# Fewer warm-up products and a drain placed elsewhere, in a kernel of attention and expert routing

## The chip, the cores and the metric

The kernel runs on one core of one Trainium2 chip. The core has five engines with instruction queues of their own: TensorE (PE in the profile; its loads of the stationary operand are PEld), VectorE (DVE), ScalarE (ACT), GpSimd (POOL) and SyncE (SP, which here only starts transfers). They wait for each other through semaphores. The metric is the time of one execution in microseconds of the device; less is better.

## The reference

A linear attention over four batches of four heads, 1088 positions and 32 features, whose output, laid out as 4352 tokens of 128 features, goes through a layer of eight experts, of which each token uses the one with the highest score.

```python
def _attn_ref(q, k, v, S1, S2):
    def phi(x):                                   # 64 features from two sketches of 8
        a = np.einsum('rd,bhsd->bhsr', S1, x)
        b = np.einsum('rd,bhsd->bhsr', S2, x)
        return np.einsum('bhsi,bhsj->bhsij', a, b).reshape(*x.shape[:-1], r * r)
    q_p, k_p = (phi(q), phi(k))
    kv = np.einsum('bhsf,bhsd->bhfd', k_p, v)
    z = np.sum(k_p, axis=2)
    num = np.einsum('bhsf,bhfd->bhsd', q_p, kv)
    den = np.einsum('bhsf,bhf->bhs', q_p, z)[..., None] + 1e-06
    return (num / den)

def _moe_ref(x, w_gate, w1, w2):                  # x: 4352 tokens x 128
    logits = x @ w_gate
    expert_idx = np.argmax(logits, axis=1)
    ...                                           # gate_w: the softmax at the chosen expert
    for e in range(E):
        mask = expert_idx == e
        out[mask] = gate_w[mask, None] * (np.maximum(x[mask] @ w1[e], 0.0) @ w2[e])
    return out
```

All in float32.

## The kernel before

The program has two parts. In the first, TensorE transposes blocks of keys and queries, multiplies them with the sketches, sums keys times values and forms the tokens; POOL scatters the tokens into a table in DRAM (`xs_dram`), sorted by expert. In the second, 34 tiles (`JMIN`) of up to 128 tokens of one expert, and up to four optional ones of two half tiles, are gathered back, go through the expert's two products (`up`, `down`) and are stored to their places in the output by POOL.

The beginning, as far as it matters here. Loads go out on two queues; meanwhile TensorE multiplies zeros:

```python
    nc.vector.memset(zeros, 0.0)
    # ... loads of the sketches, of keys, values and queries ...
    idle = bank_ps("idle")
    for i in range(12):
        nc.tensor.matmul(idle[:, 0:128], lhsT=zeros[:, 0:128], rhs=zeros[:, 0:128], start=True, stop=True)
    # ... VectorE unpacks the sketches (given as float64) into s_rep ...

    def finish_s():                       # first of the order: two transposes of the sketches
        for i in range(2):
            nc.tensor.transpose(p[:, :2 * R], in_=sT[i]..., identity=ident[:2 * R, :2 * R])
            # ... VectorE: s_cat

    def features(name, n, srcs, dst):     # T.K00, T.K01, ...: then the first blocks of keys
        def turn():
            for i, s in enumerate(srcs()):
                nc.tensor.transpose(tp[:, ts(i, 128)], in_=s, identity=ident)
            nc.scalar.copy(out=st["xT"][:, :n * 128], in_=tp[:, :n * 128])
        def project():
            # ... TensorE: xT times s_cat, ScalarE, VectorE: the 64 features
```

The weights of the experts (16 loads of 512 KB) follow on SP's queue while the first part runs.

The store of a tile, an indirect transfer that POOL issues, and the loop over the tiles (five of them are done before it):

```python
    def down(j):
        # ... TensorE: py = hT times w2 of the tile's expert
        y = y_of(j)                       # sixteen buffers
        nc.scalar.activation(y, py[:, :DM], AF.Copy, bias=0.0, scale=xg_of(j)[:, DM:DM + 1])

    def store(j):
        d = nc.gpsimd.indirect_dma_start(
            out=out[:], out_offset=bass.IndirectOffsetOnAxis(ap=to_of(j), axis=0),
            in_=y_of(j), in_offset=None, bounds_check=NTOK - 1, oob_is_err=False)

    for j in range(5, JMIN):
        o = after.get(j)                  # an optional tile beside tiles 14, 18, 22, 26
        if o is not None:
            with tc.If(runs[o - JMIN] > 0) as found:
                # ... x_in(j + 2), up(o), down(j), up(j + 1), down(o)
            with found.Else():
                # ... the same without o
            waiting += [j, o]
        else:
            # ... x_in(j + 2), up(j + 1), down(j)
            waiting.append(j)
        # ... gathers of later tiles
        for _ in range(2 if j + 1 < JMIN else JT):
            if waiting:
                store(waiting.pop(0))
        if j % 8 == 0 and j > 8 or j + 3 == JMIN:
            nc.gpsimd.drain()
```

With `JMIN` = 34 the drain stands behind the stores of tiles 16, 24, 31 and 32. In the profile `idle` is line 198, the store line 856, y line 852, the drain line 949, the branch line 915, and line 976 is the end of the program.

Of the kernel before, what the change touches and what calls it, by code (L numbers as in the profile page):

```python
# [62 lines left out]
def kernel(  # L63
# [31 lines left out]
    JMIN = NTOK // 128  # L95
# [26 lines left out]
    def bank_ps(name):  # L122
        return ps_w.tile([128, 512], FP, tag="w", name=name)
# [70 lines left out]


    idle = bank_ps("idle")
    for i in range(12):
        nc.tensor.matmul(idle[:, 0:128], lhsT=zeros[:, 0:128], rhs=zeros[:, 0:128], start=True, stop=True)  # L198


# [583 lines left out]
    def gather(j):  # L784
        n = 128 // len(tiles[j][0])
        for i, (_, at) in enumerate(tiles[j][0]):
            _, (row,) = nc.values_load_multi_w_load_instructions(
                at, engines=[mybir.EngineType.SP], min_val=0, max_val=E * NTOK - n,
                skip_runtime_bounds_check_because="the table keeps a tile within its expert's rows")
            d = nc.sync.dma_start(out=xg_of(j)[ts(i, n)].bitcast(I32), in_=xs_dram[ds(row, n), :])  # L790
            if j < JE:
                tc.declare_no_dep(d.ins, group="late", reason="late rows are in no tile of the first group")
                tc.add_to_no_dep_group("early", d.ins)
# [7 lines left out]
    def x_in(j):  # L801
        xg = xg_of(j)
        xTp = bank_ps(f"xgTp{j}")
        nc.tensor.transpose(xTp[:, :128], in_=xg[:, 0:DM], identity=ident)  # L804
        nc.scalar.copy(out=xT_of(j), in_=xTp[:, :128])  # L805
        for w1, (at, _) in zip([w1_of(j)] if j < JMIN else w1_half, tiles[j][0]):
            wo = w_offset(at, DVE)
            nc.vector.tensor_copy(out=w1, in_=w1_all[:, ds(wo, F)])  # L808
        if j >= JMIN:

            nc.vector.tensor_copy(out=w2_half, in_=w2_all[:, ds(wo, F)])

    def rows_out(j):

        to = to_of(j)
        row_id = xg_of(j)[:, DM + 1:DM + 2].bitcast(I32)
        if j < JE:
            nc.vector.tensor_copy(out=to, in_=row_id)
        else:
            nc.vector.tensor_tensor(to, row_id, tiles[j][1], ALU.bitwise_or)  # L820

    def up(j):
        xT = xT_of(j)
        ph = wide_ps(f"ph{j}")
        for c in range(NFC):
            if j < JMIN:
                nc.tensor.matmul(ph[:, ts(c, 128)], lhsT=w1_of(j)[:, ts(c, 128)], rhs=xT, start=True, stop=True)  # L827
                continue
            for i, w1 in enumerate(w1_half):
                for m in range(2):  # L830
                    nc.tensor.matmul(ph[ts(m, 64), ds(c * 128 + i * 64, 64)], lhsT=w1[:, ds(c * 128 + m * 64, 64)],  # L831
                                     rhs=xT[:, ts(i, 64)], start=True, stop=True)
        hT = hT_of(j)
        nc.scalar.activation(hT[:, 0:512], ph[:, 0:512], AF.Relu)  # L834
        if j <= 7:

            nc.scalar.activation(hT[:, 512:1024], ph[:, 512:1024], AF.Relu)
        else:
            nc.vector.tensor_scalar(hT[:, 512:1024], ph[:, 512:1024], 0.0, None, ALU.max)  # L839

    def down(j):
        hT = hT_of(j)
        wo = w_offset(tiles[j][0][0][0], PE)
        n = 128 // len(tiles[j][0])
        py = bank_ps(f"py{j}")
        for c in range(NFC):
            for i in range(128 // n):
                nc.tensor.matmul(py[ts(i, n), :DM], lhsT=hT[:, ds(c * 128 + i * n, n)],  # L848
                                 rhs=w2_half[:, ts(c, DM)] if i else w2_all[:, ds(wo + c * DM, DM)],
                                 start=(c == 0), stop=(c == NFC - 1))  # L850
        y = y_of(j)
        nc.scalar.activation(y, py[:, :DM], AF.Copy, bias=0.0, scale=xg_of(j)[:, DM:DM + 1])  # L852

    def store(j):
        y = y_of(j)
        d = nc.gpsimd.indirect_dma_start(  # L856
            out=out[:], out_offset=bass.IndirectOffsetOnAxis(ap=to_of(j), axis=0),
            in_=y, in_offset=None, bounds_check=NTOK - 1, oob_is_err=False)
        tc.declare_no_dep(d.ins, group="y", reason="every token is in one tile")
        tc.add_to_no_dep_group("y", d.ins)  # L860
# [18 lines left out]
    def piece():  # L879
        for _ in last_table:  # L880
            break
# [21 lines left out]
    for j in range(sum(name[0] == "Z" for name in begun), JMIN):  # L903
        o = after.get(j)
        if j + 4 == min(after):
            runs = []
            for i in range(NS):
                _, (v,) = nc.values_load_multi_w_load_instructions(
                    tiles["runs"][0:1, i:i + 1], engines=engines, min_val=0, max_val=2 * NS,
                    skip_runtime_bounds_check_because="a number of halves")  # L910
                runs.append(v)
        if o is not None:
            rows_out(j)
            rows_out(o)
            with tc.If(runs[o - JMIN] > 0) as found:
                x_in(j + 2)
                up(o)
                down(j)
                up(j + 1)
                down(o)  # L920
            with found.Else():
                up(j + 1)
                x_in(j + 2)
                down(j)
            waiting += [j, o]
        else:
            if j + 2 < JMIN:
                x_in(j + 2)
            if j + 1 in after:
                x_in(after[j + 1])  # L930
            rows_out(j)
            if j + 1 < JMIN:
                up(j + 1)
            for _ in range({5: 8, 6: 4}.get(j, 0)):
                piece()
            down(j)
            waiting.append(j)

        for i in range(JE, j + AHEAD + 1) if j == 6 else [j + AHEAD] if j > 6 else []:
            if i < JMIN:  # L940
                gather(i)
        if j > 8 and optional:
            gather(optional.pop(0))
        for _ in range(2 if j + 1 < JMIN else JT):
            if waiting:
                store(waiting.pop(0))
        if j % 8 == 0 and j > 8 or j + 3 == JMIN:

            nc.gpsimd.drain()  # L949

# [30 lines left out]
```

## Time and profile before

| | |
|---|---|
| time, median of 3 | 227.0 us (226.95 to 227.46) |
| span of the profiled execution | 252.5 us |
| mean granted clock of TensorE in it | 0.912 |
| TensorE busy | 214.7 us, 85% |
| VectorE, ScalarE, POOL busy | 113.8, 75.3, 84.0 us |
| moved by DMA | 23.15 MB |

The span runs from the first to the last instruction of one profiled execution; it is longer than the plain ones, which have no profile. A group of instructions is named by its line, its engine, its operation and its tiles as `out<-in`. "Issue" is idle time that no release in the profile explains. An engine's name with a q (POOLq, PEldq) is its sequencer: waits, branches and drains stand there and do not count as busy. In a table of windows each line is a stretch in us, then its length, the engine's busy time with the number of instructions, the granted clock (1.00 is full), the busy share of the DMA engines and GB/s. By the page, POOL's stores are 34 instructions of 979 ns, and 34 scatters of 1011 ns stand before them.

### The profile page before, as it was taken

What the parts mean: (1) busy time and instruction counts of PE and PEld (TensorE: products, weight loads), DVE (VectorE), ACT (ScalarE), POOL (GpSimd) and SP (SyncE); (2) the same over time, 40 slices, a digit from 0 to 9 for tenths busy, and PEclk for the clock granted to TensorE, in tenths of its full rate; (3) what the DMA queues carried; (4) which work ended last, traced back from release to release, by engine and by line L of the source; (5) the groups of instructions that cost most, each with busy time, mean ns of one, the idle gap of its engine ahead of it and who ended that gap; (6) DMA issues with size and microseconds to landing.
All of it is one profiled execution on the core that took longest, in us unless ns stands there. A gap on an engine that the chain in (4) does not pass through costs nothing.

```text
span 252.5 us, 7067 instructions
## 1 busy us (share of the span) xinstructions
PE 214.7 (85%) x2654; PEld 204.4 (81%) x2654; DVE 113.8 (45%) x310; ACT 75.3 (30%) x197; POOL 84.0 (33%) x130
## 2 busy tenths in 40 slices
PE   8998995595599895991099999999999999799990
PEld 8888993583498795990099999899999999699990
DVE  4565882361268770185081344533632555153320
ACT  2546370041145322400043323222232233132220
POOL 6440057337400084077422321304114333133322
PEclk9999999598589998696579999999999999799997
DMA  5988688888831221011112211101101111000000
GB/s 172 323 229 175 179 247 253 257 234 235 276 101 25 63 66 42 3 44 53 42 31 76 64 44 45 43 4 49 32 14 46 34 32 32 14 12 22 10 23 21
DMA packets 28180, 23.15 MB, mean 92 GB/s; under 512 B 5786, under 2 KB 26012, under 8 KB 28144
## 3 DMA queue, kind: packets, MB, share of 16 engines
q1 hardware_dynamic: 24736, 18.02, 26.1%
q0 software_dynamic: 2304, 4.50, 5.3%
q8 instruction: 25, 0.41, 0.7%
q10 hardware_dynamic: 1104, 0.13, 0.4%
q14 instruction: 11, 0.09, 0.1%
HBM read 17.61 MB, written 5.29 MB: 91 GB/s over the span
## 4 chain that ended last, share of the span: by engine, by line
PE 72%; issue 12%; another core or an unknown queue 7%; DVE 3%; ACT 2%; POOLq 1%; SPq 1%; DMA 1%; POOL 0%; DVEq 0%; ACTq 0%
PE ph L827 23%; PE py L848 22%; PE ab_K L356 4%; PE ab_Q L356 4%; PE kv L379 3%; PE nd_Q L454 3%; PE qp_Q L442 2%; PE idle L198 2%; PE tp_Q L347 2%; PE ph L831 2%; PE xgTp L804 1%; PE tp_K L347 1%; POOLq L949 1%; DMA x_rows<-xs_dram 1%
## 5 line engine op out<-in xcount | busy, mean ns | idle before, releaser
L827 PE MATMUL ph<-xgT,w 128*128 128x128 f32 x544 | 71.9, 287 | 15.6 <-ACT xgT L805 9.5
L827 PEld LDWEIGHTS ph<-xgT,w 128*128 128x128 f32 x544 | 68.1, 202 | 17.1 <-ACT xgT L805 10.7
L848 PE MATMUL py<-w_all,hT 128*128 (+1 forms) x576 | 72.5, 280 | 1.6 <-issue 1.6
L848 PEld LDWEIGHTS py<-w_all,hT 128*128 128x128 f32 (+1 forms) x576 | 68.8, 193 | 2.3 <-issue 1.8
L856 POOL DMA_INDIRECT out_dram<-y,to x34 | 33.3, 979 | 92.9 <-ACT xgT L805 61.1
L550 POOL DMA_INDIRECT xs_dram<-x_rows,row_i x34 | 34.4, 1011 | 49.1 <-DVE base_e L544 21.8
L839 DVE TENSOR_SCALAR hT<-ph 128x512 f32<-128x512 f32 x28 | 19.4, 692 | 67.0 <-ACT hT L834 55.6
L834 ACT ACTIVATE hT<-ph 128x512 f32<-128x512 f32 x36 | 21.6, 599 | 58.1 <-PE ph L827 39.6
L852 ACT ACTIVATE y<-py,x_rows 128x128 f32<-128x128 f32 x34 | 12.5, 368 | 56.1 <-PE py L848 34.7
L808 DVE COPY w<-w_all 128x1024 f32 x34 | 23.3, 691 | 10.9 <-remote 8.3
L356 PE MATMUL ab_Q<-s_cat,xT_Q 128*64 128x64 f32 x256 | 12.9, 232 | 8.0 <-issue 8.0
L356 PEld LDWEIGHTS ab_Q<-s_cat,xT_Q 128*64 128x64 f32 x256 | 10.6, 142 | 9.5 <-issue 9.5
L356 PE MATMUL ab_K<-s_cat,xT_K 128*64 128x64 f32 x256 | 11.4, 235 | 3.4 <-issue 3.1
L364 DVE TENSOR_TENSOR q_p_Q<-half_Q 128x1024 f32<-128x1024 f32 x8 | 9.7, 1224 | 10.3 <-ACT half_Q L363 10.3
L356 PEld LDWEIGHTS ab_K<-s_cat,xT_K 128*64 128x64 f32 x256 | 9.7, 146 | 4.9 <-issue 4.4
L364 DVE TENSOR_TENSOR k_p<-half_K 128x1024 f32<-128x1024 f32 x8 | 9.6, 1221 | 6.8 <-issue 4.1
L454 PE MATMUL nd_Q<-kvx,q_pT_Q 128*64 128x82 f32 x256 | 11.4, 237 | 1.4 <-issue 1.3
L454 PEld LDWEIGHTS nd_Q<-kvx,q_pT_Q 128*64 128x64 f32 x256 | 10.0, 136 | 2.7 <-issue 2.2
L230 POOL COPY v_aug<-v 128x1024 f32<-128x1024 f32 x4 | 5.5, 1386 | 19.0 <-DMA v<-in_v_dram 19.0
L804 PE MATMUL xgTp<-ident,x_rows 128*128 128x128 f32 x38 | 10.2, 286 | 0.3 <-issue 0.3
L805 ACT COPY xgT<-xgTp 128x128 f32<-128x128 f32 x38 | 9.4, 264 | 2.8 <-PE xgTp L804 1.6
L363 ACT COPY half_Q<-ab_Q 128x256 f32<-128x256 f32 x8 | 3.0, 373 | 24.4 <-PE ab_Q L356 18.3
(194 smaller groups left out, 213.6 us busy)
## 6 DMA issues: line engine op xcount, KB each, us to landing
w_all<-in_moe_w_dram SPq DMA_DIRECT2D x16, 512.0 KB
x_rows<-xs_dram SPq DMA_DIRECT2D x34, 65.0 KB
k<-in_k_dram SPq DMA_DIRECT2D x4, 512.0 KB
v<-in_v_dram SPq DMA_DIRECT2D x4, 512.0 KB
q<-in_q_dram SPq DMA_DIRECT2D x4, 512.0 KB
xs_dram<-x_rows,row_i POOLq DMA_INDIRECT x34
out_dram<-y,to POOLq DMA_INDIRECT x34
xs_dram<-zeros SPq DMA_DIRECT2D x1, 520.0 KB
```

What stands on the lines that cost most here:

```text
L356: nc.tensor.matmul(ab[ts(m, 64)].rearrange("p (g i r) -> p g i r", g=4, i=n)[:, :, i], lhsT=st["xT"][:, ds(i * 128 + m * 64, 64)], rhs=s_c ...
L364: nc.vector.tensor_tensor(f.rearrange("p g (a b) -> p g a b", a=R), half[:, :, 0:R, None].broadcast_to(shape), half[:, :, None, R:2 * R].b ...
L454: nc.tensor.matmul(nd[ts(m, 64), i, ds(hp * 2 * KC, 2 * KC)], lhsT=t[:, ds((i * NP + hp) * 128 + m * 64, 64)], rhs=kvx[bs[m]][:, hp].rearr ...
L550: d = nc.gpsimd.indirect_dma_start(out=xs_dram[:], out_offset=bass.IndirectOffsetOnAxis(ap=row_i[:, u:u + 1], axis=0), in_=x[:, u, :].bitc ...
L804: nc.tensor.transpose(xTp[:, :128], in_=xg[:, 0:DM], identity=ident)
L808: nc.vector.tensor_copy(out=w1, in_=w1_all[:, ds(wo, F)])
L827: nc.tensor.matmul(ph[:, ts(c, 128)], lhsT=w1_of(j)[:, ts(c, 128)], rhs=xT, start=True, stop=True)
L834: nc.scalar.activation(hT[:, 0:512], ph[:, 0:512], AF.Relu)
L839: nc.vector.tensor_scalar(hT[:, 512:1024], ph[:, 512:1024], 0.0, None, ALU.max)
L848: nc.tensor.matmul(py[ts(i, n), :DM], lhsT=hT[:, ds(c * 128 + i * n, n)], rhs=w2_half[:, ts(c, DM)] if i else w2_all[:, ds(wo + c * DM, DM ...
L852: nc.scalar.activation(y, py[:, :DM], AF.Copy, bias=0.0, scale=xg_of(j)[:, DM:DM + 1])
L856: d = nc.gpsimd.indirect_dma_start(out=out[:], out_offset=bass.IndirectOffsetOnAxis(ap=to_of(j), axis=0), in_=y, in_offset=None, bounds_ch ...
```

## The change

Two edits. TensorE multiplies zeros eight times at the start in place of twelve; the products fill the time until the first keys are there. And the drains of POOL among the tiles stand behind tiles 14, 22 and 30 (`JMIN - 4`) in place of 16, 24, 31 and 32, so that there are three of them, the last one four tiles from the end.

```diff
     idle = bank_ps("idle")
-    for i in range(12):
+    for i in range(8):
         nc.tensor.matmul(idle[:, 0:128], lhsT=zeros[:, 0:128], rhs=zeros[:, 0:128], start=True, stop=True)
...
             if waiting:
                 store(waiting.pop(0))
-        if j % 8 == 0 and j > 8 or j + 3 == JMIN:
+        if j in (14, 22, JMIN - 4):

             nc.gpsimd.drain()
```

## The prediction

> **What bounds the kernel now.** I read the two ends of the program, because the change touches only those and the drains between, and I read them in this order: the chain of waits, then the timeline around its last pieces, then the first nine microseconds of TensorE, then TensorE's clock. The profiled execution lasts 252.5 us and the plain ones 227.0: in the profile TensorE ran at half clock in several stretches (mean clock 0.912), so I take pieces of a few microseconds from it and no totals. TensorE is the bound of the body: the page has it busy for 85% of the span, and the chain is 72% TensorE. At the very end the chain leaves it. This is the end of the chain of waits of the kernel before (start in us, length, what):
>
> ```profile
> 237.72 0.37 ACT y L852
> ...
> 238.36 0.97 POOL out_dram L856
> ...
> 241.81 1.20 POOLq L949
> ...
> 245.38 1.20 POOLq L949
> 246.58 1.37 issue
> ...
> 248.58 1.19 POOLq L976
> ```
>
> From tile 30's store at 238.36 the chain runs through POOL's own queue: two drains of line 949, then the drain that ends the program (line 976). No matmul is in the last 14 us of it. The timeline of the same stretch shows what that means (start, length, engine, line, operation, and in brackets the idle time before it and what ended it):
>
> ```profile
> 241.40 0.37 ACT L852 ACTIVATE y<-py,x_rows 128x128 f32<-128x128 f32 x1 [1.13 <-PE py L848]
> 242.04 0.97 POOL L856 DMA_INDIRECT out_dram<-y,to  x1 [2.71 <-ACT y L852]
> ...
> 245.62 0.97 POOL L856 DMA_INDIRECT out_dram<-y,to  x1 [2.61 <-ACT y L852]
> 246.76 0.37 ACT L852 ACTIVATE y<-py,x_rows 128x128 f32<-128x128 f32 x1 [1.42 <-PE py L848]
> 248.80 0.97 POOL L856 DMA_INDIRECT out_dram<-y,to  x1 [2.21 <-issue]
> ```
>
> The stores of tiles 31 and 32 were released by their y; the store of tile 33, the last, was not: its y was ready at 247.13 and it started at 248.80, "issue". The line of the drains, asked for alone in three stretches (duration ns, then starts), says what held it:
>
> ```profile
> L949 POOLq DRAIN  x1: 5062/5062/5062, 212.2 to 212.2; - x1
> L949 POOLq DRAIN  x1: 2837/2837/2837, 241.8 to 241.8; - x1
> L949 POOLq DRAIN  x1: 2546/2546/2546, 245.4 to 245.4; - x1
> ```
>
> The drain after tile 31 ends at 241.81 + 2.84 = 244.65, before tile 32's y (245.34), so it costs nothing. The drain after tile 32 ends at 245.38 + 2.55 = 247.93, later than tile 33's y by 0.80, and POOL then takes another 0.87 to start the store. The start of TensorE, its timeline and the three lines of what it needs first:
>
> ```profile
> 1.06 5.49 PE L198 MATMUL idle<-zeros 128*128 128x128 f32 x24 [1.06 <-DVE zeros L154]
> 6.48 0.31 PE L321 MATMUL sTp<-ident,s_rep 16*128 16x16 f32 x2
> 6.72 1.09 PE L347 MATMUL tp_K<-ident,k 128*128 128x128 f32 x8
> ...
> L311 DVE TENSOR_TENSOR s_rep<-rest,expo_at x1: 310/310/310, 4.6 to 4.6; 16x128 f32<-16x128 f32 x1
> ...
> L347 PEldq EVENT_SEMAPHORE  x1: 51/51/51, 5.5 to 5.5; - x1
> ```
>
> The 12 products (24 records: two passes each in f32) run back to back from 1.06 to 6.55. The sketch operands are ready at 4.56 + 0.31 = 4.87, and the queue's wait for the keys ends at 5.5. So the first transpose of keys, at 6.72, waits for zeros, not for keys: some 1.2 us. Last, TensorE's busy time and granted clock in windows of 3.413 us counted from 6.55:
>
> ```profile
> 37.27:40.68 3.41, 2.44 (x49) 1.00 0.81 221
> 40.68:44.09 3.41, 1.44 (x16) 1.00 0.95 273
> 44.09:47.51 3.42, 1.30 (x11) 0.50 0.85 261
> 47.51:50.92 3.41, 2.67 (x50) 0.50 0.74 238
> 50.92:54.33 3.41, 3.41 (x64) 1.00 0.91 247
> ```
>
> A window 42% busy is followed by half clock, one 78% busy at half clock by full clock.
>
> [...] a product on zeros takes 421 ns a pass before 6.55, a transpose of the same shape 273 ns after. [...]
>
> **The change, part by part.**
>
> *The last drain.* Tile 32's drain goes. The last store then starts as the two before it did: y ready to store started was 242.04 - 241.77 = 0.27 and 245.62 - 245.34 = 0.28, so 247.13 + 0.28 = 247.41 in place of 248.80, 1.39 us earlier. From the store's start to the end of the span is 252.5 - 248.80 = 3.7 us, made of its landing and the program's closing waits; I keep it. The closing drain now has three stores behind it, not one: 2837 against 2546 ns for eight against one says 0.04 a store, 0.1 in all, and beside other closing waits. I count **1.35 us**.
>
> *The other drains.* After tile 24 becomes after tile 22, after 16 becomes after 14, after 31 becomes after 30. They hold POOL alone, and POOL's only work is the stores, which nothing waits for until the end (sixteen y buffers): the one at 212.2 lasted 5.06 us, and the body ran on. The drain behind tile 30 starts near 238.1 (a drain's record starts 0.23 before the store ahead of it, as 241.81 against 242.04), takes about 2.84, and with 0.87 to restart POOL is free at 241.8; tile 31's store is due at 242.04. It fits with 0.2 to spare, and a miss would not move tile 33. **0 us.**
>
> *The products.* Four products are eight passes. At half clock their spacing is (6.13 - 1.06)/23, some 0.213 to 0.22 us, so they are 1.7 us: TensorE would be done at about 4.85. Then the two sketch transposes at 4.9, then an idle gap to the keys at 5.5. The transposes of keys move from 6.72 to about 5.5, but in this execution's phase the clock rises only at 6.55, so the first four take twice as long: fourth started at 5.5 + 3 x 0.213 = 6.15, ended some 0.35 later, ScalarE's copy from 6.5 in place of 7.41. That is 0.9 us. With an early phase the products themselves speed up and the twelve are over near 5.5, so the gain is nearly 0; with a late phase it is 1.2. I take 0.7 as the mean. Does the clock still rise as early? The gap and the sketch transposes leave the window busy for some 85 to 90%, over the 78% that sufficed at 47.51, so I say yes. Of the 0.7 not all reaches the end: from 38 to 69 us TensorE is busy for only 19.26 of 31 us while the weight loads run, and the gathers come at fixed distances behind the loads. I choose 0.7 of it: **0.5 us**.
>
> Sum: 1.35 + 0 + 0.5 = 1.85, so 227.0 - 1.85 = 225.15, say **225.1 us**.
>
> **The rivals.**
>
> *The clock stays low longer.* If the gap at 4.9 to 5.5 spoils the window, the rise comes 3.41 us later, and about 3.4 us of early work at half speed costs up to 1.7 us: 0.9 gained, 1.7 lost, plus 1.35 at the end, 226.5. For it: the products exist for nothing else. Against: the window that sufficed was less busy than this one would be.
>
> *The start is hidden.* The shift is eaten by the loads of keys, values and queries and by the fed-late stretch to 69 us. For it: DMA share is 0.82 over the first 40 us. Against: TensorE is busy for 36.79 of those 40. Then only the end counts: 225.65.
>
> *The drain moved is a wait moved.* The closing drain could take over what the removed one waited for, so that the end stands where it stood: 226.5 with the start alone. Against: the removed drain waited for tile 32's store, out by 247.93 (2.31 after its start at 245.62); the closing drain waits for tile 33's, out by 247.41 + 2.31 = 249.7, so it waits for tile 32's without waiting longer.
>
> [...]
>
> **Range and chances.** The end's 1.35 is the firm part; the start adds 0 to 1.2 or takes 0.8; [...] the times before spread over 0.5. I give **223.7 to 226.7**. Faster by 2% needs under 222.46[...]: 0.04. Slower by 2% needs over 231.5: 0.02. Within: 0.94.
>
> **What would show it.** Right: no record of line 949 after the one near tile 30, the last store released by y and starting about 0.3 us after it, the span ending about 3.7 us later; 16 records of products, the first transpose of keys at about 5.5. Wrong: a last store that again starts more than a microsecond after its y, a closing drain of over 3 us, keys that land after 6.5, a clock that rises only around 10 us, or a new long branch on TensorE.

## The result, and the profile after

The changed kernel takes **224.11 us** (median of 4 runs, 223.3 to 224.83), the kernel before, in the same comparison, 226.97 (226.39 to 227.46). The ratio is **0.9874, 95% interval 0.9828 to 0.9919**: 2.86 us less by the medians, 1.84 to 3.9 by the interval. 225.1 was predicted, within 223.7 to 226.7, from a sum of 1.85: 1.35 at the end and 0.5 at the start. This program runs near 225 us or near 252 us whichever version it is, the profile of before and all experiments being of the longer kind and the profile of after (221.5 us) of the shorter, so that totals are compared only with the kernel before of the same series, and from profiles only stretches of a few microseconds. The profiling is not what made the span of before longer than the plain executions: the profiled execution of the changed kernel, 223.3 us, is the fastest of its four.

**The end.** The timeline of the last three stores in the changed kernel:

```profile
212.47 0.97 POOL L856 DMA_INDIRECT out_dram<-y,to  x1 [2.71 <-ACT y L852]
...
215.40 0.37 ACT L852 ACTIVATE y<-py,x_rows 128x128 f32<-128x128 f32 x1 [1.13 <-PE py L848]
216.04 0.97 POOL L856 DMA_INDIRECT out_dram<-y,to  x1 [2.60 <-ACT y L852]
217.19 0.37 ACT L852 ACTIVATE y<-py,x_rows 128x128 f32<-128x128 f32 x1 [1.42 <-PE py L848]
217.83 0.97 POOL L856 DMA_INDIRECT out_dram<-y,to  x1 [0.82 <-ACT y L852]
```

The last store stood at "issue" before; now y releases it as it does the two ahead of it. y is ready at 217.19 + 0.37 = 217.56, the store starts at 217.83, 0.27 later (before: 247.13 and 248.80, 1.67), and the program ends 221.5 - 217.83 = 3.67 us after that (before 3.7). The drains of line 949, in the whole program and in its last stretch, and the closing ones of line 976 (count, shortest/median/longest ns, first and last start; the line after the dots is the closing drain of the kernel before):

```profile
L949 POOLq DRAIN  x3: 2887/3469/6042, 142.6 to 208.6; - x3
L949 POOLq DRAIN  x1: 2887/2887/2887, 208.6 to 208.6; - x1
L976 POOLq DRAIN  x3: 46/107/2644, 217.6 to 221.2; - x3
...
L976 POOLq DRAIN  x3: 46/108/2532, 248.6 to 252.2; - x3
```

The last drain among the tiles ends at 208.56 + 2.89 = 211.45, and tile 31's store at 212.47 is released by its y: the moved drain holds nobody. The closing drain is 2644 ns, against 2532 before.

**The start.** The timeline of TensorE in the changed kernel, its first pieces:

```profile
1.06 3.78 PE L198 MATMUL idle<-zeros 128*128 128x128 f32 x16 [1.06 <-DVE zeros L154]
...
5.57 1.94 PE L347 MATMUL tp_K<-ident,k 128*128 128x128 f32 x8 [0.31 <-DMA k<-in_k_dram]
7.44 3.42 PE L356 MATMUL ab_K<-s_cat,xT_K 128*64 128x64 f32 x64
10.79 0.33 PE L347 MATMUL tp_kr<-ident,k_rem 128*128 128x128 f32 x1
```

The transposes of keys are released by the keys, 1.15 us earlier than before (5.57 against 6.72). But eight of them take 1.94 us where they took 1.09, and the 64 projections 3.42. The projections still start 0.6 earlier than before (7.44 against 8.05); the remainder's transpose, after them, comes 0.7 later (10.79 against 10.06). The first change on the record of TensorE's clock is the rise to full at 10.42; passes 128 columns wide started every 0.213 us before it and every 0.109 after. The chain of waits of the changed kernel from 25 to 75 us says what an early microsecond of TensorE could have bought:

```profile
25.27 3.80 DMA k<-in_k_dram
...
29.12 4.60 DMA q<-in_q_dram
...
33.73 4.32 DMA w_all<-in_moe_w_dram
...
64.17 4.21 DMA w_all<-in_moe_w_dram
...
69.60 4.21 DMA x_rows<-xs_dram
...
73.86 0.48 PE xgTp L804
```

It is transfers from end to end, each behind the one before it, and TensorE waits 10.8 us for the first gathered rows. The load that opens the row starts at 25.27, and at 25.26 in the kernel before. The chain puts a product of TensorE in front of it (line 454, to 25.27), but by SyncE's own waits of 20 to 25.5 us it waited 4.6 us for the transfer of zeros into the table, in both kernels the same. Some of the loads in between start up to 2 us sooner than in the profile of before, but the last one starts at 68.40, and at 68.54 there. In the profile of the kernel before, the chain from 25 to 90 us is another one: TensorE's lines with 20% of "issue" between them. There the first gathers do not follow the loads; SyncE's waits from 70 to 82 us (in total, times, longest) are one:

```profile
SPq L787 <- DVE first_row L612: 9.6, 1, 9.6
```

It waits for VectorE to work out where the tiles' rows begin. So the prediction's "the gathers come at fixed distances behind the loads" holds in the profile of the changed kernel (68.40 and 69.60) and not in that of before.

### The profile page after: what moved, and what is told of

It is laid out like the page before. It is cut to its first block, busy times and chain, and to the rows that moved or that the text cites. A ratio compares the mean times of both kernels' runs of the same rounds, so it can differ in the third digit from the quotient of the medians.

```text
span 221.5 us, 7050 instructions
## 1 busy us (share of the span) xinstructions
PE 200.5 (90%) x2646; PEld 193.1 (87%) x2646; DVE 115.0 (52%) x310; ACT 75.1 (34%) x197; POOL 85.0 (38%) x130
## 4 chain that ended last, share of the span: by engine, by line
PE 62%; DMA 23%; issue 8%; POOL 1%; POOLq 1%; DVE 1%; ACT 1%; SPq 1%; DVEq 0%; ACTq 0%
PE py L848 24%; PE ph L827 24%; DMA w_all<-in_moe_w_dram 16%; DMA k<-in_k_dram 4%; PE ab_K L356 2%; DMA q<-in_q_dram 2%; PE xgTp L804 2%; DMA x_rows<-xs_dram 2%; PE ph L831 2%; PE nd_Q L454 2%; PE tp_K L347 1%; PE ab_Q L356 1%; POOL out_dram L856 1%; PE kv L379 1%; PE tp_Q L347 1%
## 5 line engine op out<-in xcount | busy, mean ns | idle before, releaser
L848 PE MATMUL py<-w_all,hT 128*128 (+1 forms) x576 | 70.1, 276 | 0.0
L827 PE MATMUL ph<-xgT,w 128*128 128x128 f32 x544 | 67.3, 278 | 2.6 <-issue 1.7
L827 PEld LDWEIGHTS ph<-xgT,w 128*128 128x128 f32 x544 | 64.2, 194 | 3.6 <-issue 2.1
L848 PEld LDWEIGHTS py<-w_all,hT 128*128 128x128 f32 (+1 forms) x576 | 66.7, 189 | 0.4
L856 POOL DMA_INDIRECT out_dram<-y,to x34 | 34.5, 1014 | 73.9 <-ACT xgT L805 49.4
L804 PE MATMUL xgTp<-ident,x_rows 128*128 128x128 f32 x38 | 10.3, 289 | 10.8 <-DMA x_rows<-xs_dram 10.8
L804 PEld LDWEIGHTS xgTp<-ident,x_rows 128*128 128x128 f32 x38 | 5.4, 145 | 11.8 <-DMA x_rows<-xs_dram 11.0
L230 POOL COPY v_aug<-v 128x1024 f32<-128x1024 f32 x4 | 4.2, 1039 | 17.0 <-DMA v<-in_v_dram 17.0
L356 PE MATMUL ab_K<-s_cat,xT_K 128*64 128x64 f32 x256 | 10.0, 242 | 0.0
L356 PE MATMUL ab_Q<-s_cat,xT_Q 128*64 128x64 f32 x256 | 9.2, 223 | 0.7 <-issue 0.7
L445 ACT COPY q_pT_Q<-qp_Q 128x512 f32<-128x512 f32 x16 | 8.5, 592 | 3.6 <-PE qp_Q L442 3.6
```

The source lines that it names most:

```text
L356: nc.tensor.matmul(ab[ts(m, 64)].rearrange("p (g i r) -> p g i r", g=4, i=n)[:, :, i], lhsT=st["xT"][:, ds(i * 128 + m * 64, 64)], rhs=s_c ...
L856: d = nc.gpsimd.indirect_dma_start(out=out[:], out_offset=bass.IndirectOffsetOnAxis(ap=to_of(j), axis=0), in_=y, in_offset=None, bounds_ch ...
```

## The experiments

Theory A is the prediction's: the drain behind tile 32 alone is worth 1.35 us, the moved drains nothing, the four products some 0.5. Theory B: what is won at the start is lost again (the clock stays low, or the loads hide it), so the drain is all. Theory C: the closing drain takes over the wait.

**One part of the change at a time.** The drains alone, three times:

```diff
-        if j % 8 == 0 and j > 8 or j + 3 == JMIN:
+        if j in (14, 22, JMIN - 4):
```

> Twelve products as before, drains behind tiles 14, 22 and 30 as in the changed kernel. Both ends (the prediction): 1.35 us less than before, the last store about 0.3 us after its y. Start hidden behind the loads: the whole 2.9 us of the changed kernel comes from the drains, so 2 to 3 us less. [...]

> Twelve products, drains as changed. Start hidden behind the loads: the same time as the changed kernel within 0.5 us, the clock rising before 7 us and yet nothing gained from it. Both ends (the prediction): 0.5 us more than the changed kernel.

> Twelve products, drains as changed, beside the kernel with eight products and the drains of before. About 1.4 us less than before; some 1.4 us less than the kernel with eight products and the old drains if the start gives nothing, 0.9 us less if the prediction holds.

Only tile 32's drain away, the others where they were, twice:

```diff
-        if j % 8 == 0 and j > 8 or j + 3 == JMIN:
+        if j in (16, 24, 31):
```

> Twelve products, drains behind tiles 16, 24 and 31: only the drain behind tile 32 is gone. The wait of the last store alone: 1.35 to 1.4 us less than before, all that the drains give. If the moved drains matter too: less than what the kernel with all the drains moved gains.

> Twelve products, only the drain behind tile 32 gone. The wait of the last store alone: the same time as with all drains moved, within 0.5 us, some 1.4 us less than before. If the moved drains matter too: more time than with all drains moved, by what the changed kernel gained over 1.4 us.

The products alone, twice:

```diff
-    for i in range(12):
+    for i in range(8):
```

> Eight products, drains behind tiles 16, 24, 31 and 32 as before. Both ends (the prediction): 0.5 us less than before. Start hidden behind the loads: the same as before within 0.3 us, and the transfers of keys, values and weights start at the same times as with twelve. [...]

> Eight products with the drains of before, timed more often. Start hidden or lost: the same as before within 0.5 us, or up to 1 us more, because with eight products the clock rises some 3.4 us later. Both ends (the prediction): 0.5 us less.

The kernel before and the changed kernel once more, unedited:

> The kernel before once more, for a profile without the half-clock stretches. All theories: about 227 us. Start hidden behind the loads: TensorE stands still some 10 us for the first gathered rows in this profile too, and the gathers start at the same time as in the changed kernel, near 69.6 us. Both ends: the gathers start some 0.5 us later than in the changed kernel.

> The changed kernel once more beside others. If the chip runs the kernel before at some 227 us: about 224.1 again. If at some 252 us, as in the last four: some 1.4 to 2 us less than before. In the profile the clock of TensorE rises after 9 us, as in the two earlier profiles with eight products, and the transfers of the first 26 us start when they do with twelve.

Measured, each beside the kernel before of the same series (times are medians of all executions in us: 22 of each kernel, six of "products only, 1", of which one took 353.61, and 44 to 75 of the kernel before; "y to store" is the last tile's, from the timeline):

| kernel | time | before | ratio of the executions within 1.5% of their kernel's fastest, 95% interval | y to store |
|---|---|---|---|---|
| drains only, 1 | 250.98 | 252.8 | 0.9991 (0.9952 to 1.003) | 0.27 |
| drains only, 2 | 253.28 | 254.14 | 0.9947 (0.9907 to 0.9987) | 0.27 |
| drains only, 3 | 251.85 | 252.61 | 0.9968 (0.993 to 1.0005) | 0.27 |
| tile 32's only, 1 | 251.15 | 252.8 | 0.9993 (0.9948 to 1.0037) | 0.27 |
| tile 32's only, 2 | 252.05 | 254.14 | 0.9927 (0.9886 to 0.9969) | 0.27 |
| products only, 1 | 252.94 | 252.8 | 1.0125 (1.0029 to 1.022) | 1.67 |
| products only, 2 | 252.63 | 252.61 | 1.004 (1.001 to 1.007) | 1.66 |
| before again | 252.24 (one execution) | | | 1.68 |
| changed again | 253.5 | 254.14 | 0.9952 (0.9905 to 1.0) | 0.27 |

The profile of "before again" was to show when the gathers start with twelve products in an execution near 225 us; it took 252.24 us, so this stayed unanswered. The last column is the sharpest. The timeline's last two lines with the drains moved (drains only, 1):

```profile
243.54 0.37 ACT L852 ACTIVATE y<-py,x_rows 128x128 f32<-128x128 f32 x1 [1.42 <-PE py L848]
244.18 0.97 POOL L856 DMA_INDIRECT out_dram<-y,to  x1 [0.82 <-ACT y L852]
```

with tile 32's drain alone away (tile 32's only, 1):

```profile
242.52 0.37 ACT L852 ACTIVATE y<-py,x_rows 128x128 f32<-128x128 f32 x1 [1.42 <-PE py L848]
243.16 0.97 POOL L856 DMA_INDIRECT out_dram<-y,to  x1 [0.81 <-ACT y L852]
```

and with the products alone (products only, 1), where tile 32's drain is kept:

```profile
245.50 0.37 ACT L852 ACTIVATE y<-py,x_rows 128x128 f32<-128x128 f32 x1 [1.42 <-PE py L848]
247.54 0.97 POOL L856 DMA_INDIRECT out_dram<-y,to  x1 [2.22 <-issue]
```

The gap between y and store is 1.66 to 1.68 us in every kernel with a drain behind tile 32 and 0.27 in every one without: **1.40 us**, and the five runs that change drains only lie 1.82, 0.86, 0.76, 1.65 and 2.09 below the kernel before by their medians, 1.44 on the mean. Single intervals reach from 0.9 us slower to 2.9 us faster; it is the trace that gives the size. Where the other drains stand makes no difference that these runs show: moved and unmoved, the medians are 250.98 and 251.15 in one series, 253.28 and 252.05 in the other. The products alone bring nothing: their medians are 0.14 and 0.02 above, their ratios a little over 1, and the interval of the second, with 22 executions, leaves no room for a gain. That falls on A's 0.5 and speaks for B, as far as these runs, all near 252 us, go.

**One product.** To see whether less of a warm-up costs more, the changed kernel with one product:

```diff
-    for i in range(8):
+    for i in range(1):
```

> One product in place of eight, drains as changed: nothing warms TensorE before the keys come. Start hidden behind the loads: the same time as the changed kernel within 0.7 us, though TensorE is at half clock until some 10 us. Warming matters: over 1 us more than the changed kernel.

253.75 against 254.14 of before, ratio 0.9934 (0.9877 to 0.9991). With the same drains in the same series, twelve products took 253.28 and eight 253.5: eleven products fewer are some half a microsecond, under what these runs tell apart. The clock rose at 10.72 us and the end hardly noticed. So in these runs nothing that was done at the start shows at the end. What swallows it these profiles do not name: their chain from 25 to 90 us runs through TensorE, with 19 to 25% of it "issue".

**No drains at all.** If a drain in the wrong place costs, is the best number none? The changed kernel without its drain lines:

```diff
-        if j in (14, 22, JMIN - 4):
-
-            nc.gpsimd.drain()
```

> Eight products and no drain among the tiles at all. If a drain settles every transfer since the last one, at 0.046 to 0.058 us each: the closing drain has 72 stores and scatters behind it, lasts some 2.4 + 3.3 to 4.2 us, and the end stands 2 to 3.5 us later than in the changed kernel. If the drains among the tiles are only waits: the same as the changed kernel.

256.79 (six executions) against 252.61: ratio 1.021 (1.014 to 1.028), 4.2 us more than before by the medians. From the last store to the end of the span it is 251.6 - 243.86 = 7.7 us, where the changed kernel has 3.67: 4.1 more, past the 2 to 3.5 that were expected. The drains of the program's end in this kernel (its lines stand three further up), POOL's and SyncE's:

```profile
L973 POOLq DRAIN  x3: 40/108/7158, 243.6 to 251.3; - x3
L973 SPq DRAIN  x3: 7/7/13, 246.7 to 251.0; - x3
```

The closing drain lasts 7158 ns with 72 transfers of POOL since the start and no drain between, against 2644 with 3 since the last drain in the changed kernel: (7158 - 2644)/69 = 0.065 us for each, an estimate from these two. SyncE comes to its own first drain at 246.7, but POOL's ends at 243.6 + 7.2 = 250.8 and the program with it. So without the drains among the tiles the closing one is 4.5 us longer, and the last of those, until 211.45 in the changed kernel, stood where POOL's next store came only at 212.47. The data were out long before: the last packet of POOL's queue ended at 245.76, 5.0 us before the drain did (in the changed kernel at 219.72, 0.5 before). What the drain does in that time no profile says. Nor is the number of transfers all: with ten since the last drain, the one behind tile 24 in the kernel before lasted 5062 ns and the one behind tile 22 in the changed kernel 3469.

**The clock.** In the changed kernel it rose at 10.42 us, not near 6.55. Theories for that: transposes do not count as activity, or the window was not busy enough. The test takes the products out and puts 48 transposes of zeros behind the making of the identity:

```diff
-    for i in range(8):
-        nc.tensor.matmul(idle[:, 0:128], lhsT=zeros[:, 0:128], rhs=zeros[:, 0:128], start=True, stop=True)
...
+    for i in range(48):
+        nc.tensor.transpose(idle[:, 0:128], in_=zeros[:, 0:128], identity=ident)
```

> In place of the products 48 transposes of zeros, from some 2.7 us on, when the identity is there; they run for some 10 us at half clock. Transposes count for the clock as products do: it rises by 9.5 us, after the first full window of 3.41 us. Transposes do not count, or too little: it rises only after the projections of the keys, later than 12.7 us. The time itself is some microseconds more for either.

One execution: 252.51 us. TensorE's timeline in it:

```profile
2.71 6.76 PE L202 MATMUL idle<-ident,zeros 128*128 128x128 f32 x48 [2.71 <-POOL mask L204]
...
9.63 1.09 PE L347 MATMUL tp_K<-ident,k 128*128 128x128 f32 x8
```

The spacing of the transposes falls from 0.213 to 0.109 us at 5.43: with transposes alone the clock rose, 2.72 us after their start. The windows rest on a step that the traces show: after the first rise, 6.55 us in the kernel before and 10.42 in the changed one, the clock changes there at 44.09, 50.92, 61.16, 71.40 and seven times more, here at 65.03 and 78.69, each a whole number of 3.413 us later (11, 13, 16 and 19; 16 and 20). The windows of the run with transposes, of 3.41 us, up to and behind the rise (length, TensorE's busy time and instructions, clock, DMA share, GB/s; the clock column stands at 1.00 until the first change on record, so the speed is read from the durations):

```profile
2.02:5.43 3.41, 2.71 (x13) 1.00 0.74 232
5.43:8.84 3.41, 3.41 (x33) 1.00 1.13 320
```

and those of the changed kernel up to its rise at 10.42:

```profile
0.18:3.59 3.41, 2.53 (x12) 1.00 0.20 42
3.59:7.01 3.42, 3.11 (x15) 1.00 1.13 333
7.01:10.42 3.41, 3.41 (x59) 1.00 1.14 318
```

2.71 us busy came before the rise in the one; 3.11 in the other did not bring it. So the profile's busy time does not tell the two apart. It holds the sketch transposes, which are 16 wide, and the modelled tails of the products. If only passes that follow each other without a gap are counted, from start to start and without the two narrow ones, the changed kernel's window has the products until 4.64 and the keys from 5.57: (4.64 - 3.59) + (7.01 - 5.57) = 2.49 us, 73%; the 48 transposes have 5.43 - 2.71 = 2.72, 80%. Counted so, the windows of the first ten microseconds fall in two: those up to 76% were followed by half clock, those at 80% and over by full clock. (The 76% is the first window of "tile 32's only, 2", (3.64 - 1.06)/3.41.) But this count was found after the fact, and a later window goes against it. In the kernel with one product, behind a pause of 9.6 us, passes of 128 columns stand back to back from 127.46 to the end of this window, again 2.72 us or 80%, and the clock stayed at half for another window:

```profile
126.77:130.18 3.41, 2.72 (x13) 0.50 0.06 19
```

So neither the busy share nor the count of passes gives a line, the prediction's 78% included, and what the clock counts stays open. The times of the rise stand by themselves: eight products fill 3.6 us, hardly more than one window, and whether an early rise hangs on how the windows happen to lie was not shown. With eight it rose at 10.42, 10.04, 9.14, 5.24 and 5.27 us, with one at 10.72; with twelve, in seven profiles, between 4.03 and 7.05.

## Why the prediction was right, and where it was wrong

**The last drain (1.35): right.** The start of the last store against its y went from 1.67 to 0.27, the stretch from store to end stayed (3.7 and 3.67), the closing drain grew by 0.11 where 0.1 was said. Measured as a gap: 1.40.

**The other drains (0): right.** The drain's end (208.56 + 2.89 = 211.45) and the restart fit ahead of tile 31's store (212.47), and leaving the others where they stood shows no difference.

**The products (0.5): wrong.** The step that failed is "The gap and the sketch transposes leave the window busy for some 85 to 90%, over the 78% that sufficed at 47.51, so I say yes." The busy share was about as said, 3.11 of 3.42 or 91%, and the clock did not rise: the busy share in the profile did not foretell it, and the two windows compared were not made of the same instructions (the one at 47.51 holds projections and products of keys and values, lines 356 and 379). So the transposes of keys ran all eight at half speed, not the first four. The 0.7 for an early and a late phase was an estimate, of a spread that the trace of before alone does not show; with twelve products the rise came at 4.03 to 7.05 us in seven profiles, and the products themselves took 4.40 us in "before again" and 5.49 in the profile of before. The second failure is "I choose 0.7 of it": no gain at the start showed at the end. Products alone came out 0.14 and 0.02 longer, one product no different from twelve. In the changed kernel's profile the chain gives a reason, the loads up to 68.40 us, of which the last starts when it did before; that is read from one chain, and in all the other profiles the first gathers wait 2.5 to 11.1 us for VectorE's row numbers, behind the last load.

**The rivals.** "The start is hidden" (225.65) is the one that held in kind, with the reason it gave, the loads, seen in the changed kernel's chain alone. The argument against it, TensorE busy for 36.79 of the first 40 us, misled: with all that work ahead of it, the load that opens the row of transfers starts at 25.26 before and 25.27 after. "The clock stays low longer" came true in four of the six profiles with eight products or one (9.14 to 10.72 us), but its cost does not show at the end either. "The drain moved is a wait moved" is refuted (2532 and 2644 ns). The argument against it took a drain to end when the store ahead of it is out. In the trace of before the drains behind the stores of tiles 32 and 33 ended at 247.93 and 251.11, each 2.31 after the start of its store and 0.42 after its last packet (247.51 and 250.69); that a drain waits for this was an estimate from such figures, and in the kernel without drains it ended 5.0 after. A new long branch, named as a sign against the prediction, did not come: TensorE's six branch records of line 915 last 71 to 3507 ns, and 74 to 3694 in the kernel before.

**The size, left open.** Of the 2.86 us measured, 1.4 are shown. The other 1.46 (0.4 to 2.5 by the interval) are not. In the experiments the changed kernel was only 0.64 below the kernel before (0 to 2.4 by its interval), so the rest could not be studied there; a gain at the start that counts only in runs near 225 us would be a candidate, but the chain through the loads speaks against it, and no run tests it. 225.1 lay within a microsecond of the result partly by luck: 0.5 for which no run gives a sign stood in for something that was not found.

## What to carry to other kernels

The drain of POOL that ended at 211.45, before its next store at 212.47, held nothing; the one that ended at 247.93 in the kernel before, 0.80 after the last tile's y, cost 1.4 us. So put the last drain where that slack is, and do not leave it out: without any the closing drain here took 7.2 us in place of 2.6. Before early work is shortened, look for the first transfer behind it that starts at the same time in any case, as the load at 25.27 (25.26 before) did here: no gain ahead of it showed at the end, though TensorE was busy for 36.79 of the first 40 us. And a few warm-up products are a gamble: with eight the clock rose at 5.2 us in one run and at 10.4 in another.

## What the runs showed of the hardware

- A drain of POOL's queue behind indirect transfers lasted 2532 ns with one transfer since the last drain (before), 2644 with three (changed), 7158 with seventy-two and no drain before it (no drains). With seventy-two the last packet had ended 5.0 us before the drain did. With ten it lasted 5062 ns in the kernel before and 3469 in the changed one, so the number of transfers is not all.
- 48 transposes of zeros in f32, with no product ahead of them, were followed by a rise of the clock 2.72 us after their start (at 5.43 us); their spacing went from 0.213 to 0.109 us.
- In the traces of both kernels every change of TensorE's clock lies a whole number of 3.413 us after the first rise.
- A window 91% busy by the profile (3.11 of 3.42 us, changed kernel) was not followed by a rise of the clock, one of 79% (2.71 of 3.41 us, 48 transposes) was; of two windows with passes of 128 columns back to back for 80% of their length (2.72 us), one was followed by full clock (48 transposes) and one by half (one product).
